# Putting w2 and the later loads behind the DMA transposes of block 1, and letting the scans read their start in place

## The chip, the core and the metric

The kernel runs on one core of a Trainium2 chip. The metric is the device time of one execution in microseconds (us); lower is better. "Span" below is the part of it from the first to the last instruction in the profile; the time is 1.8 to 2.7 us longer than the span in every run listed here. PE is the matmul engine, ACT the scalar engine, DVE the vector engine, POOL is GpSimd, and SP is SyncE, which here only issues DMAs. "Slow" means over 1.5% above the fastest run of the same kernel; every other run is "fast". "Clock" is the share of its full clock that PE was granted, 1.0 being all of it.

## The reference, cut to what matters

```python
xn = layernorm(x)                          # x: [1, 2048, 512] bf16
# A: state-space model. Bu = xn @ B_bar^T (complex), then a scan over 2048 steps
h = Lam_bar * h + Bu[:, t]                 # for each t
ya = 2 * Re(hseq @ C^T) + xn * Dskip
# B: SwiGLU, F = 1792
yb = (silu(xn @ w1) * (xn @ w3)) @ w2
out = x + ya + yb
```

## The kernel before

The 2048 rows are cut into four blocks of 512. For each block the kernel needs xnT, the normalised rows transposed. For blocks 1 to 3 the transposes are DMAs, four of 128 rows each. PE multiplies xnT with w1 and w3 ("gate/up", `glu`), and with B (`bu`). DVE runs the scans. The order of the queue on SP is the order of these calls:

```python
def bulk_loads():                       # called while block 0 starts
    ...
    load_w(4 * P, MID * P)              # slices of w1 and w3
    load_x(1)
    nc.sync.dma_start_transpose(out=bt[:, 0], in_=A_B_re)
    nc.sync.dma_start_transpose(out=bt[:, 1], in_=A_B_im)
    load_w(MID * P, F)
    nc.sync.dma_start_transpose(out=ct_in[:, :, 0, :], in_=A_C_re)
    nc.sync.dma_start_transpose(out=ct_in[:, :, 1, :], in_=A_C_im)
    nc.sync.dma_start(out=w2_sb, in_=...)          # 1792 KB
    nc.sync.dma_start(out=dskip_row, in_=...)

def late_loads():
    load_x(2)
    load_x(3)

def ln_transpose(b, cl):                # blocks 1 to 3
    nc.sync.dma_start_transpose(out=xnT_blk[b][:, :, cl*P:(cl+1)*P], in_=xn_blk[b][:, cl, :])
...
for t in ln1b:                          # normalise block 1 and issue its transposes
    bg.add(*t, ("ln", 1))
bg.add(0.2, params_w)
gate = glu(0)
bg.flush(("ln", 1))
gate()
late_loads()
...
gate = glu(1)                           # first reader of block 1's xnT
```

`bg` is a list of small tasks for the other engines, handed out between PE's groups of matmuls; `flush(key)` empties it up to the last task with that key. The scans of a block start from the last state of the block before. For two of the three hand-overs that state was first copied:

```python
if b == 0: init = 0.0
elif b - 1 in FAST: init = ends[b - 1, hf][:, 2*j + ri : 2*j + ri + 1]
else: init = act_blk[b - 1][:, k_state(pt, ri), TBLK - 1:TBLK]
...
gp.tensor_copy(out=ends[b, hf], in_=act(b)[:, k:k + 4, TBLK - 1])   # after block b's states are done
```

## Time and profile before

| | before |
|---|---|
| time, median of 3 runs | 210.19 us (210.09 to 210.56) |
| the profiled run | 212.91 us, span 210.9 us, state slow |
| PE, DVE, ACT busy | 96%, 86%, 61% of the span |

From the timeline of PE, kernel before (start, length, engine, line, operation, output<-inputs, shapes, count; in brackets the idle time before it and what ended it):

```profile
33.73 5.13 PE L506 MATMUL gu_ps<-xnT,w_sb 128*128 128x512 bf16 x23
41.29 4.02 PE L506 MATMUL gu_ps<-xnT,w_sb 128*128 128x512 bf16 x11 [2.43 <-DMA xnT<-xn]
```

PE ends block 0's gate/up matmuls at 38.86 us (33.73 + 5.13) and stands 2.43 us, until block 1's transposes have landed. The windows of one microsecond show the clock in the third column from the right (PEclk), then DMA share and GB/s:

```profile
39.00:40.00 1.00, 0.00 (x0) 0.00 (x0) 0.96 (x3) 0.50 (x1) 0.00 (x0) 1.00 1.32 259
40.00:41.00 1.00, 0.00 (x0) 0.00 (x0) 1.00 (x2) 0.00 (x0) 0.00 (x0) 0.96 0.80 135
41.00:42.00 1.00, 0.71 (x2) 0.28 (x3) 1.00 (x2) 0.00 (x0) 0.00 (x0) 0.50 0.85 267
42.00:43.00 1.00, 1.00 (x4) 0.34 (x3) 1.00 (x2) 0.00 (x0) 0.00 (x0) 0.50 1.04 310
43.00:44.00 1.00, 1.00 (x4) 0.40 (x3) 1.00 (x2) 0.60 (x1) 0.00 (x0) 0.50 1.04 356
44.00:45.00 1.00, 1.00 (x6) 0.41 (x4) 0.97 (x2) 0.24 (x1) 0.00 (x0) 0.84 0.27 95
```

From shortly before 41 us PE was granted half its clock for 3.4 us (0.08 + 3 + 0.32), a loss of at most 1.7 us: for the first 0.38 us of it PE was still waiting. The queue explains the wait. From the timeline of SP (the length is how long SP was held by issuing, not how long the transfer took: w2, L175, held SP for 0.58 us and landed 9.8 us after its issue):

```profile
20.92 5.74 SPq L173 DMA_TRANSPOSE ct<-in_A_C_re_dram  x1
26.70 2.24 SPq L174 DMA_TRANSPOSE ct<-in_A_C_im_dram  x1
28.99 0.58 SPq L175 DMA_DIRECT2D w_sb<-in_B_w_dram  x1
29.62 1.45 SPq L176 DMA_DIRECT2D dskip_row<-in_A_Dskip_dram  x1
31.17 8.21 SPq L239 DMA_TRANSPOSE xnT<-xn  x4
39.43 1.12 SPq L154 DMA_DIRECT2D x_blk<-in_A_x_dram  x2
```

The normalised rows of block 1 are ready at 25.8 us, but the last of their four transposes is issued at 38.16 and lands at 41.16. The scans, from the page's groups (busy us, mean ns of one, idle before):

```profile
L462 DVE TENSOR_TENSOR_SCAN u<-rho,ends,u 128x512 bf16<-128x512 f32 x16 | 19.6, 1268 | 0.1
L462 DVE TENSOR_TENSOR_SCAN u<-rho,act,u 128x512 bf16<-128x512 f32 x8 | 9.7, 1263 | 0.0
```

### The profile page before, as it was taken

The numbers are of one execution on the slowest core, as the hardware profiler recorded it, in microseconds if no ns is written. First come the engines' busy times: TensorE is split into PE (matmuls) and PEld (weight loads), VectorE is DVE, ScalarE is ACT, GpSimd is POOL, SyncE is SP. The second block draws the span as 40 slices with busy tenths as digits, with TensorE's granted clock in tenths as the row PEclk, the third lists the DMA queues.
The fourth block names the chain that finished last, engine by engine and source line by source line (L and its number), as shares of the span: only waits on it lengthen the run. The fifth ranks groups of instructions, "written<-read, shape, count | busy, mean of one in ns | idle before, by whom it ended". The sixth has DMA issues, their size and how long they took to land.

```text
span 210.9 us, 3257 instructions
## 1 busy us (share of the span) xinstructions
PE 203.2 (96%) x1251; PEld 116.7 (55%) x1251; DVE 181.8 (86%) x236; ACT 128.8 (61%) x257; POOL 28.8 (14%) x51
## 2 busy tenths in 40 slices
PE   8999999599999999999999799999999999999994
PEld 2964444144444444444444344788644448888893
DVE  4789699999893699999999589897999999996932
ACT  4799787369999995727995987401266673011010
POOL 3340399100000003120106000200000000000000
PEclk9999999879999999999999999999999999999999
DMA  5998999930000000440000220000100000001011
GB/s 168 276 177 174 321 238 319 168 133 0 0 3 0 0 0 0 51 120 31 2 0 0 53 50 0 0 28 25 51 3 0 0 0 0 28 25 52 26 39 40
DMA packets 26103, 13.71 MB, mean 65 GB/s; under 512 B 15720, under 2 KB 26088, under 8 KB 26088
## 3 DMA queue, kind: packets, MB, share of 16 engines
q1 hardware_dynamic: 25512, 13.21, 27.5%
q10 hardware_dynamic: 576, 0.30, 0.5%
q8 instruction: 10, 0.16, 0.3%
q14 instruction: 5, 0.04, 0.1%
HBM read 7.74 MB, written 2.10 MB: 47 GB/s over the span
## 4 chain that ended last, share of the span: by engine, by line
PE 74%; DVE 11%; ACT 7%; DMA 3%; POOL 2%; issue 1%; DVEq 0%
PE gu_ps L506 30%; PE gu_ps L697 11%; PE bu_ps L423 8%; PE y_ps L697 7%; PE gu_ps L763 6%; PE bu_ps L697 5%; DMA xnT<-xn 3%; PE bu_ps L190 2%; PE gu_ps L769 2%; DVE u L462 2%; ACT u L516 2%; ACT g L515 1%; DVE act L523 1%; ACT xn L274 1%; DVE stats L211 1%
## 5 line engine op out<-in xcount | busy, mean ns | idle before, releaser
L506 PE MATMUL gu_ps<-xnT,w_sb 128*128 128x512 bf16 x424 | 94.0, 383 | 3.5 <-DMA xnT<-xn 2.4
L506 PEld LDWEIGHTS <-w_sb 128*128 128x128 bf16 x424 | 41.7, 99 | 54.7 <-issue 6.2
L515 ACT ACTIVATE g<-gu_ps 128x512 bf16<-128x512 f32 x55 | 33.1, 602 | 14.2 <-PE gu_ps L506 14.1
L516 ACT ACTIVATE u<-gu_ps 128x512 bf16<-128x512 f32 x55 | 33.3, 605 | 7.5 <-PE gu_ps L506 6.6
L697 PEld LDWEIGHTS <-act 128*128 128x128 f16 x341 | 32.4, 98 | 4.3 <-DVE act L729 0.2
L423 PE MATMUL bu_ps<-xnT,bt 128*128 128x512 bf16 x128 | 28.8, 379 | 0.4 <-DMA xnT<-xn 0.3
L523 DVE TENSOR_TENSOR act<-g,u 128x1024 f16<-128x1024 bf16 x28 | 19.1, 680 | 7.8 <-ACT u L516 7.8
L425 ACT ACTIVATE u<-bu_ps 128x512 bf16<-128x512 f32 x32 | 19.1, 596 | 5.9 <-PE bu_ps L423 5.8
L423 PEld LDWEIGHTS <-bt 128*128 128x128 bf16 x128 | 12.4, 98 | 16.3 <-issue 1.0
L462 DVE TENSOR_TENSOR_SCAN u<-rho,ends,u 128x512 bf16<-128x512 f32 x16 | 19.6, 1268 | 0.1
L763 PE MATMUL gu_ps<-w_sb,act 128*128 128x512 bf16 x56 | 12.4, 379 | 0.0
L447 DVE TENSOR_TENSOR u<-u,tabe 128x2048 bf16<-128x2048 bf16 x8 | 9.8, 1221 | 0.1
L444 DVE TENSOR_TENSOR p<-u,tabe 128x2048 bf16<-128x2048 bf16 x8 | 9.8, 1220 | 0.1
L467 DVE TENSOR_TENSOR p<-u,tabe 128x2048 bf16<-128x2048 bf16 x8 | 9.8, 1220 | 0.1
L474 DVE TENSOR_TENSOR act<-act,p 128x2048 f16<-128x2048 f16 x8 | 9.7, 1216 | 0.1
L451 DVE TENSOR_TENSOR u<-u,p 128x2048 bf16<-128x2048 bf16 x8 | 9.8, 1219 | 0.0
L470 DVE TENSOR_TENSOR act<-u,tabe 128x2048 f16<-128x2048 bf16 x8 | 9.7, 1216 | 0.0
L462 DVE TENSOR_TENSOR_SCAN u<-rho,act,u 128x512 bf16<-128x512 f32 x8 | 9.7, 1263 | 0.0
L282 ACT ACTIVATE xn<-x_blk,acc,rstd_all 128x512 bf16<-128x512 bf16 x8 | 6.2, 811 | 5.3 <-POOL acc L279 5.3
L462 DVE TENSOR_TENSOR_SCAN u<-rho,u 128x512 bf16<-128x512 f32 x8 | 9.2, 1208 | 0.1
L763 PEld LDWEIGHTS <-act 128*128 128x128 f16 x56 | 5.5, 98 | 6.6
L710 ACT ACTIVATE bu_ps<-y_ps 128x256 f32<-128x256 f32 x3 | 1.1, 368 | 11.9 <-PE y_ps L697 11.9
(138 smaller groups left out, 264.0 us busy)
## 6 DMA issues: line engine op xcount, KB each, us to landing
out_dram<-xn SPq DMA_DIRECT2D x15, 128.0 KB, 1.7
w_sb<-in_B_w_dram SPq DMA_DIRECT2D x1, 1792.0 KB, 9.8
x_blk<-in_A_x_dram SPq DMA_DIRECT2D x3, 512.0 KB, 5.5
w_sb<-in_B_w_dram SPq DMA_DIRECT2D x2, 768.0 KB, 6.7
w_sb<-in_B_w_dram SPq DMA_DIRECT2D x4, 256.0 KB, 3.7
w_sb<-in_B_w_dram SPq DMA_DIRECT2D x2, 512.0 KB, 7.6
xnT<-xn SPq DMA_TRANSPOSE x12, 3.0
x_blk<-in_A_x_dram ACTq DMA_DIRECT2D x2, 64.0 KB
```

Of the source, the lines that this page charges most:

```text
L423: nc.tensor.matmul(out=ps, lhsT=bt[:, ri, dt, pt * P:(pt + 1) * P], rhs=xnT_blk[b][:, dt, :], start=(dt == 0), stop=(dt == NDT - 1))
L425: nc.scalar.activation(out=u[:, j, ri, :], in_=ps, func=ACT.Copy)
L444: nc.vector.tensor_tensor(out=st["p"], in0=st["g"], in1=tabe[:, psl, 1:3, :], op=ALU.mult)
L447: nc.vector.tensor_tensor(out=st["g"], in0=st["g"], in1=tabe[:, psl, 0:1, :].to_broadcast(FULL), op=ALU.mult)
L451: nc.vector.tensor_tensor(out=st["g"], in0=st["g"], in1=st["p"][:, :, ::-1, :], op=ALU.subtract)
L462: nc.vector.tensor_tensor_scan(out=v, data0=rho[:, pt:pt + 1].to_broadcast([P, TBLK]), data1=v, initial=init, op0=ALU.mult, op1=ALU.add)
L506: nc.tensor.matmul(out=ps[:, tsl], lhsT=w[:, dt, f * P:(f + 1) * P], rhs=xnT[:, dt, tsl], start=(dt == 0), stop=(dt == NDT - 1))
L515: nc.scalar.activation(out=g16[:, f % 2, :], in_=g_ps, func=ACT.Silu)
L516: nc.scalar.activation(out=u16[:, f % 2, :], in_=u_ps, func=ACT.Copy)
L523: nc.vector.tensor_tensor(out=act(b)[:, k0:k1 + 1:k1 - k0, :], in0=g16, in1=u16, op=ALU.mult)
L697: nc.tensor.matmul(out=out, lhsT=left[:, k, :], rhs=right[k][:, cols], start=(start and k == 0), stop=(k == NK - 1), skip_group_check=True)
L763: nc.tensor.matmul(out=tiles[cl], lhsT=act_blk[b][:, k_gate(f), cl * P:(cl + 1) * P], rhs=w2_sb[:, f, :], start=False, stop=False, skip_gr ...
```

## The change

The intent: in the trace of before the first reader of dskip starts at 54.6 us and the first of w2 at 58.0 us, so let the four transposes of block 1 go ahead of it; and drop the GpSimd copies of the last states. The core of the diff:

```diff
@@ bulk_loads / late_loads
         nc.sync.dma_start_transpose(out=ct_in[:, :, 1, :], in_=A_C_im)
+
+    def late_loads():
         nc.sync.dma_start(out=w2_sb, in_=B_w2.rearrange("(t p) d -> p t d", p=P))
         nc.sync.dma_start(out=dskip_row, in_=A_Dskip.partition_broadcast(P))
-
-    def late_loads():
         load_x(2)
         load_x(3)
@@ scan
-                if b == 0:
-                    init = 0.0
-                elif b - 1 in FAST:
-                    init = ends[b - 1, hf][:, 2 * j + ri:2 * j + ri + 1]
-                else:
-                    init = act_blk[b - 1][:, k_state(pt, ri), TBLK - 1:TBLK]
+                init = 0.0 if b == 0 else act_blk[b - 1][:, k_state(pt, ri), TBLK - 1:TBLK]
@@ post_c
-                if b in FAST and b + 1 < NBLK:
-                    ends[b, hf] = lnp.tile([P, 4], FP16, name="ends", bufs=4)
-                    k = k_state(2 * hf)
-                    gp.tensor_copy(out=ends[b, hf], in_=act(b)[:, k:k + 4, TBLK - 1])
@@ (cut: scans get their own task key, and y_fast flushes it before act is overwritten)
+        if p == 0:
+            bg.flush(("scan", b + 1))
@@ main
     for t in ln1b:
         bg.add(*t, ("ln", 1))
+    bg.add(0.0, late_loads, ("ln", 1))
     bg.add(0.2, params_w)
     gate = glu(0)
     bg.flush(("ln", 1))
     gate()
-    late_loads()
```

Apart from GpSimd's four copies, and the place from which sixteen scans read their start, the programs differ in the order of SP's queue alone. PE, DVE and ACT keep their order.

## The prediction

> **What bounds the kernel now.** The page gives PE 96% busy, DVE 86%, ACT 61%; the chain that ended last is 74% PE. So the time is PE's work plus the places where PE waits or runs slowly. The largest lies between block 0's and block 1's gate/up matmuls. The timeline shows PE idle 2.43 us there (38.86 to 41.29), released by the DMA transposes of block 1 (xnT<-xn). One-microsecond windows then show the granted clock at 0.96, 0.50, 0.50, 0.50, 0.84 from 40 to 45 us: 3.4 us at half speed, which costs half of that, 1.7 us. The chain agrees: the 112 matmuls of block 1 take 25.83 us, those of block 3 24.17 us. The stall costs 2.43 + 1.7 = 4.1 us. [...]
>
> **Why PE waits there.** The normalised x is ready at 25.8 us (timeline of DVE). On SyncE's queue the transposes come after w2 (1792 KB, issued 28.99, 9.8 us to land) and dskip. The first transpose's issue starts at 31.17 and takes 3.85 us; the others take 1.29, 1.57 and 1.22. The last lands at 41.16. Elsewhere too a transpose behind plain copies is slow to issue (9.40, 5.74 us), one behind a transpose is not (2.34, 2.24 us for the big ones).
>
> **What the change does.** The instruction order differs on SyncE only: the four transposes go before w2, dskip and the x loads. GpSimd loses four 128x4 copies; the scans read their start in place.
>
> - Transposes: behind the C transposes, first issue at about 29.0; at 1.2 to 1.6 us each the last is issued at 33 to 34 and lands, at 3.0 us, at 36 to 37. PE wants it at 38.86. The stall goes, with about 2 us to spare, and the half clock with it.
> - Delayed loads: w2, dskip, x2, x3 should land by about 47 us; the first reader (dskip, DVE, now 54.6 us) would come at about 53.
> - Scans: idle before them is 0.1 us; a scan takes 1268 ns from the copy, 1263 ns in place. Worth 0.
>
> **How much stays.** All 4.1 us lie on the chain. DVE is full from 41 to 54 us and uses PE's stall to catch up; its idle time from 53 to 68 us is 0.16 + 0.37 + 0.76 + 2.76 = 4.05 us, just what it must absorb; another 1.78 us follows at 72. The three gate buffers leave over 1 us before ACT would wait. ACT has almost no slack in block 1 (0.6 + 0.6 + 0.7 us busy each 1.73 us). I take off 0.1.
>
> **Prediction.** 210.2 - 4.0 = 206.2 us, 8 in 10 between 205.4 and 207.2. Two per cent is 206.0, so nearly a toss: faster 0.40, same 0.59, slower 0.01.
>
> **What would show it.** The last transpose of block 1 landing before 38.5 us; no PE wait over 0.3 us near 38.9; clock 1.0 from 38 to 46 us; block 1's 112 matmuls in about 24.2 us; DVE idle near zero from 41 to 63 us; block 1 ending near 63 us; later pieces of the chain 4 us earlier, unchanged in length; scans still about 1265 ns.
>
> **What would make it wrong.** The first transpose still issuing slowly (a stall of 0.5 to 1.5 us remains, perhaps without the half clock); DVE's lag filling the gate buffers and holding ACT and PE in block 1; a second clock drop at a later wait, such as the 1.1 us one near 116 us.

## The result, and the profile after

| | before | after |
|---|---|---|
| time, median of 4 runs | 210.14 us (209.93 to 210.56) | 209.06 us (208.91 to 209.37) |
| ratio of fast runs | | 0.9948, 95% interval 0.9928 to 0.9968 |
| the profiled run | 212.91 us, span 210.9, slow | 209.37 us, span 207.5, fast |

A ratio here is the mean time of one kernel's fast runs over the mean of the other's fast runs of the same rounds, so it isn't quite the ratio of the medians. The change is a gain of 0.5%, where 2% had been expected, and 209.06 lies outside the predicted 205.4 to 207.2.

Yet the profile after shows almost everything that was predicted. Timelines of SP and PE, changed kernel:

```profile
24.63 2.41 SPq L174 DMA_TRANSPOSE ct<-in_A_C_im_dram  x1
27.15 6.56 SPq L239 DMA_TRANSPOSE xnT<-xn  x4
33.76 0.57 SPq L177 DMA_DIRECT2D w_sb<-in_B_w_dram  x1
34.39 0.92 SPq L178 DMA_DIRECT2D dskip_row<-in_A_Dskip_dram  x1
35.35 2.20 SPq L154 DMA_DIRECT2D x_blk<-in_A_x_dram  x2
```

```profile
33.66 8.58 PE L497 MATMUL gu_ps<-xnT,w_sb 128*128 128x512 bf16 x38
```

The transposes go first; the trace's landing records have the last of them at 34.94 us, 4.7 us before PE wants it at 39.66. PE runs through without a gap. Two of the windows, and the stretch that was DVE's worry:

```profile
40.00:41.00 1.00, 1.00 (x6) 0.41 (x5) 0.97 (x3) 0.73 (x2) 0.00 (x0) 1.00 1.09 325
42.00:43.00 1.00, 1.00 (x7) 0.45 (x5) 1.00 (x2) 1.00 (x3) 0.00 (x0) 1.00 1.04 365
41.00:63.00 22.00, 21.89 (x101) 9.96 (x102) 21.83 (x23) 21.27 (x39) 0.00 (x0) 1.00 0.17 51
```

The clock is 1.00, PE is busy 21.89 of 22 us, DVE 21.83 of 22: it has used up its idle time, as predicted, and holds nobody. The scans:

```profile
L456 DVE TENSOR_TENSOR_SCAN u<-rho,act,u 128x512 bf16<-128x512 f32 x24 | 29.3, 1268 | 0.0
```

One thing is different from before: early, at 9.8 us, PE waits for a slice of the weights, which the profiled run of before did not.

```profile
9.79 0.40 PE L528 MATMUL bu_ps<-xnT,w_sb 128*128 128x128 bf16 x4 [0.78 <-DMA w_sb<-in_B_w_dram]
```

So the two profiles differ by 3.3 us of span and the median times by 1.1 us. The profile of before is of a slow run, that of after is not, and the two must not be compared. That is the first thing to look into.

### The profile page after: what moved, and what is told of

The parts are those of the page before. It is cut to its first block, busy times and chain, and to the rows that moved or that the text cites. A ratio compares the mean times of both kernels' runs of the same rounds, so it can differ in the third digit from the quotient of the medians.

```text
span 207.5 us, 3235 instructions
## 1 busy us (share of the span) xinstructions
PE 200.8 (97%) x1237; PEld 116.0 (56%) x1251; DVE 181.6 (87%) x236; ACT 128.8 (62%) x257; POOL 25.5 (12%) x47
## 4 chain that ended last, share of the span: by engine, by line
PE 84%; ACT 6%; DMA 5%; POOL 1%; issue 1%; DVE 1%; ACTq 0%; POOLq 0%
PE gu_ps L497 39%; PE gu_ps L690 11%; PE bu_ps L422 11%; PE y_ps L690 7%; PE gu_ps L756 6%; PE bu_ps L690 6%; DMA w_sb<-in_B_w_dram 2%; PE gu_ps L762 2%; DMA x_blk<-in_A_x_dram 2%; ACT xn L274 1%; ACT u L424 1%; DMA xnT<-xn 1%; ACT u L507 1%; ACT g L506 1%; POOL rstd_all L278 1%
## 5 line engine op out<-in xcount | busy, mean ns | idle before, releaser
L497 PE MATMUL gu_ps<-xnT,w_sb 128*128 128x512 bf16 x415 | 91.7, 379 | 1.6 <-ACT g L506 1.1
L456 DVE TENSOR_TENSOR_SCAN u<-rho,act,u 128x512 bf16<-128x512 f32 x24 | 29.3, 1268 | 0.0
L703 ACT ACTIVATE gu_ps<-gu_ps 128x256 f32<-128x256 f32 x3 | 1.1, 368 | 11.7 <-PE gu_ps L690 11.7
```

The lines of the kernel that those rows point to most:

```text
L456: nc.vector.tensor_tensor_scan(out=v, data0=rho[:, pt:pt + 1].to_broadcast([P, TBLK]), data1=v, initial=init, op0=ALU.mult, op1=ALU.add)
L497: nc.tensor.matmul(out=ps[:, tsl], lhsT=w[:, dt, f * P:(f + 1) * P], rhs=xnT[:, dt, tsl], start=(dt == 0), stop=(dt == NDT - 1))
```

## The experiments

Theory A: the profile of before was no typical run. Its DMAs ran late, so the wait was long and the half clock followed; a typical run of before loses only about 1 us. Rival B: the wait is 2.4 us in every run, only the half clock is missing in fast ones, and the changed kernel gives 1.3 us back elsewhere. Rival C: part of the gain comes from the scans.

### e1: the kernel before, unchanged, in a fast run

No edit.

> The kernel before, unchanged, for profiles and clocks of fast runs (the profile that the prediction was read from was a run of 212.9 us, the median is 210.1). Theory A (the profile before was not a typical run: there the stream of DMAs ran about 2.3 us late before the changed part began, so the wait at 38.9 us was long and the half clock followed): a fast run has clock near 1.0, no half-clock stretch of 3.4 us, PE's wait for the transposes of block 1 is 0.3 to 1.5 us, time 210.1. Rival B (the wait is about 2.4 us in fast runs too, only the half clock is missing, and the changed kernel gives 1.3 us back elsewhere): PE's wait there is 2.1 to 2.7 us at clock 1.0.

Measured: 209.72 us (209.03 to 211.38, 6 runs), all fast, clocks 0.998 to 1.0. The profiled run took 209.96 us, with a span of 207.9 us at clock 1.0. Timelines of PE and SP:

```profile
29.79 9.44 PE L506 MATMUL gu_ps<-xnT,w_sb 128*128 128x512 bf16 x43
39.86 5.34 PE L506 MATMUL gu_ps<-xnT,w_sb 128*128 128x512 bf16 x24 [0.62 <-ACT u L516]
```

```profile
25.46 2.22 SPq L174 DMA_TRANSPOSE ct<-in_A_C_im_dram  x1
27.73 0.58 SPq L175 DMA_DIRECT2D w_sb<-in_B_w_dram  x1
28.35 1.31 SPq L176 DMA_DIRECT2D dskip_row<-in_A_Dskip_dram  x1
29.77 8.18 SPq L239 DMA_TRANSPOSE xnT<-xn  x4
```

PE's gap is 0.62 us and the clock stays up. The profile puts the gap down to ACT's u, which ran from 39.27 to 39.88 us; but in the changed kernel the same u ran from 39.69 to 40.29 us while PE went on without a gap. The last transpose, issued at 36.72, landed after 3.0 us at 39.72, and PE went on at 39.86, 0.14 us later (0.13 us in the slow run, 41.16 to 41.29). Here w2 was issued at 27.73, in the slow run at 28.99, and PE arrived 0.4 us later. Theory A holds on this run, and B's 2.1 to 2.7 us is not there. The windows at the wait, with the clock third from the right:

```profile
39.00:40.00 1.00, 0.38 (x3) 0.13 (x2) 0.98 (x2) 0.60 (x2) 0.00 (x0) 1.00 0.51 116
40.00:41.00 1.00, 1.00 (x6) 0.45 (x5) 0.99 (x1) 0.08 (x1) 0.00 (x0) 1.00 1.07 379
```

The same program's ratio to itself in these rounds was 0.9987 (0.9938 to 1.0035), which shows how far noise alone can move a ratio.

The traces allow a stricter test. PE loads its weights 1251 times in the same order in both kernels, so the same load can be found in each trace. Work it out for three landmarks (times from the trace's weight-load records, us):

| trace | first 512-column load | block 0 after `bu` + all gate/up of block 1 | from `bu` of block 1 to the end of the span | span |
|---|---|---|---|---|
| before (slow) | 12.53 | 38.61 | 144.12 | 210.85 |
| e1, before (fast) | 12.90 | 35.32 | 144.10 | 207.91 |
| after | 13.32 | 34.53 | 144.08 | 207.53 |

Between the first two columns lie 15.59 us in all three. So all differences sit in two places: how early the first weights let PE start, and the stretch with the wait. 34.53 us is that stretch without a wait: the slow run of before loses 4.08 us in it, as the prediction had it, and the fast run loses 0.79. The changed kernel gives nothing back later: B's second half falls as well. (The last stretch is not always that constant. In the traces of e5, e8 and e10 it takes 143.73 to 143.75 us, 0.35 us less. In e8, which is the changed kernel once more, the difference begins where `bu` of block 2 waits for block 2's transposes.)

### e2 and e3: the two halves of the change, one at a time

e2 is the kernel before with only the load order changed (the first and the last part of the diff above). e3 has only the scans and the copies changed.

> Only the loads moved behind the transposes; the GpSimd copies of the last states stay. Theory A: the whole gain, 209.0 to 209.2 us (ratio 0.9945 to 0.996), PE's wait at 39 us gone. Rival C (part of the gain is from the scans): 209.5 us or more.

> Only the scans read the last states in place, loads as before. Theory A: as before, 210.0 to 210.3 us (ratio 0.999 to 1.001), scan mean 1260 to 1270 ns. Rival C: 209.7 us or less.

Measured: e2 took 209.12 us (208.68 to 209.52), ratio 0.9948 (0.9903 to 0.9993), the whole of the gain; its stretch is 34.53 us, as in the changed kernel. e3 took 210.28 us (208.29 to 213.58, two of six runs slow), ratio of the fast runs 0.9957 (0.9893 to 1.0022). That interval is too wide to tell anything, and its point misses the expected 0.999 to 1.001; leaving out the two slow runs also flatters it. The trace decides in its place: from `bu` of block 1 on, where the scans in question run, e3 takes 144.10 us, like e1. The in-place read is worth nothing on PE's path, and C falls. e3 has the old load order, so its trace is a second fast one of that order: PE waits 1.01 us there, and the stretch with the wait takes 35.70 us, 1.17 more than without a wait.

```profile
40.75 9.44 PE L497 MATMUL gu_ps<-xnT,w_sb 128*128 128x512 bf16 x43 [1.01 <-DMA xnT<-xn]
```

e3's own spread shows what the old load order does: spans of 206.5, 206.5, 207.1, 208.8, 209.6 and 211.2 us, the last at clock 0.992. So the half clock does come in the old order, now and then: in this run and in the profiled run of before, and in none of the 39 runs that are counted below.

### e4 and e9: a larger dose of the old order

```diff
         nc.sync.dma_start(out=dskip_row, in_=A_Dskip.partition_broadcast(P))
-
-    def late_loads():
         load_x(2)
         load_x(3)
...
     gate()
-    late_loads()
```

Against the kernel before, the loads of x blocks 2 and 3 (1 MB) also go ahead of the transposes.

> The reverse of the change, as a dose: the loads of x blocks 2 and 3 (1 MB, about 3.2 us at the 320 GB/s seen in this stretch) also go before the transposes. Theory A: the wait at 39 us grows to 3.5 to 5 us, and now the half clock of 3.4 us follows in most runs (1.7 us): 214 to 216 us. If a long wait by itself does not bring the half clock: 212.8 to 213.8 us at clock 1.0. Rival B: the wait is about 5.6 us.

> e4 again, for a count: there the half clock followed the 3.8 us wait in two of four runs. [...] again some runs at clock 0.992 and span 211 to 212, the others at 1.0 and 209.5 to 210.2; both kinds seen.

Measured: e4 213.02 us (212.28 to 214.21, 4 runs), e9 215.43 us (212.00 to 216.51, 6 runs, three of them slow). PE's wait in e4's profiled run, and two windows of it:

```profile
42.42 3.91 PE L504 MATMUL gu_ps<-xnT,w_sb 128*128 128x512 bf16 x11 [3.78 <-DMA xnT<-xn]
```

```profile
41.00:42.00 1.00, 0.00 (x0) 0.00 (x0) 1.00 (x2) 0.00 (x0) 0.00 (x0) 0.91 0.82 149
43.00:44.00 1.00, 1.00 (x4) 0.29 (x2) 1.00 (x1) 0.00 (x0) 0.00 (x0) 0.50 0.00 0
```

The wait grows with what is put ahead. The ten runs fall into three kinds: clock 1.0 with spans of 209.8, 209.9 and 210.0 us; clock 0.992 with 211.1, 211.8, 212.3 and 212.8; clock 0.984 with 213.5, 214.3 and 214.5. The steps fit one and two half-clock stretches of 1.7 us, though only the 0.992 kind has a trace. e4's median came out below the expected 214 to 216 us, as half of its runs had no half clock; five of e9's six spans (212.3 to 214.5 us) are above the expected 211 to 212, three of them with what looks like two stretches. And the half clock is not fixed by the length of the wait: e9's profiled run waited 3.17 us and kept its clock, the slow run of before waited 2.43 us and lost it.

```profile
41.91 4.26 PE L504 MATMUL gu_ps<-xnT,w_sb 128*128 128x512 bf16 x19 [3.17 <-DMA xnT<-xn]
```

The clock records of the traces say more about when. All changes of clock lie a whole number of steps of 3.413 us after the first rise to the full clock in the same trace: 34.134 us (10 steps) in the slow run of before, 37.547 us (11) in e4, 204.800 us (60) in e9, where PE's work was over. The half clock in the slow run of before lasted 3.413 us, one step. Cut each trace into windows at these steps. The clock fell at the end of a window in which PE had stood for 2.05 us (slow run of before, window ending at 40.91) or 3.19 us (e4, ending at 41.83). e9's wait of 3.17 us fell across the boundary at 40.59, 1.84 us in one window and 1.32 in the next, and the clock stayed. In the ten traces with clock records (all but e1 and e3, where no change was recorded) the clock fell after every window with 2.05 us idle or more and after none with 1.84 us or less. So in these traces it is the idle time within one window that counts, and where a wait falls decides. (The ends of matmuls in the profile are modelled. All these idle times may be about 0.2 us too short, an estimate from e1's gap of 0.62 us, which cost 0.79 us.)

### e5 and e10: keep PE busy in the wait

```diff
     gate()
+    spin = ps_bu.tile([P, TBLK], FP32, name="bu_ps")
+    for _ in range(14):
+        nc.tensor.matmul(out=spin, lhsT=ones[:, 0:P], rhs=ones, start=True, stop=True)
```

This goes on top of e4; the dummy results are read by nobody.

> The dose kernel e4 (x blocks 2 and 3 also ahead of the transposes) with 14 dummy matmuls (3.0 us) on PE in the wait. In e4 two of four runs had the half clock (spans 211.8 and 211.1 us), two had not (209.8, 209.9). If the half clock comes from PE standing idle: no run at 0.992, all spans 209.3 to 210.4 us, time 211.6 to 212.8. If it comes from something else (the DMAs, the phase of the run alone): spans near 211.5 us again in about half the runs.

> e5 again, for a count: with the dummy matmuls in the wait none of four runs had the half clock. If idleness of PE is what brings it, none of these six has it either (all spans 209.3 to 210.6 us); if the four were luck, about three of six at 0.992.

Measured: 212.62 us (212.28 to 212.88, 4 runs) and 212.75 us (211.70 to 213.75, 6 runs). In e5's trace the transposes come as late as in e4 (PE goes on at 42.51 us, there at 42.42), but PE's gap is 0.74 us:

```profile
38.55 3.22 PE L805 MATMUL bu_ps<-const-bfloat16-1.0 128*128 128x512 bf16 x14
42.51 7.71 PE L504 MATMUL gu_ps<-xnT,w_sb 128*128 128x512 bf16 x34 [0.74 <-DMA xnT<-xn]
```

Not one of the ten runs has a clock below 1.0, against seven of ten without the dummies. (Some of e10's spans, up to 211.2 us, are above the expected 210.6: the wait itself varies.) The last comparison is within the same rounds for e9 and e10: five of six runs against none of six. The DMAs issued were the same; so in these runs it is PE standing idle that brings the half clock. It also says what the dummies are worth: they keep the clock, not the time of the wait, and removing the wait is better.

### e6: is it the place in the queue, or the bytes?

```diff
+    def load_w2():
+        nc.scalar.dma_start(out=w2_sb, in_=B_w2.rearrange("(t p) d -> p t d", p=P))
     def late_loads():
-        nc.sync.dma_start(out=w2_sb, in_=B_w2.rearrange("(t p) d -> p t d", p=P))
         nc.sync.dma_start(out=dskip_row, in_=A_Dskip.partition_broadcast(P))
...
+    bg.add(0.0, load_w2)
     for t in ln1b:
         bg.add(*t, ("ln", 1))
```

This is the changed kernel with w2 in ACT's DMA queue, issued at 20.53 us. In SP's queue nothing but transposes stands ahead of block 1's from 19.8 us on.

> The changed kernel, but w2 alone is issued on ACT's DMA queue, at about 20 us, so it is in flight together with the C transposes and ahead of the block-1 transposes in time, but not ahead of them in SyncE's queue. If only the place in the queue counts: the last block-1 transpose is done by 36 us, no PE wait, spans as e8. [...] the transposes of C and of block 1 finish 3 to 6 us later than in the changed kernel (33 to 34.4 us by packets), 37 to 40 us, and PE waits 0 to 1.5 us.

(The second case is that w2's bytes delay the transposes although they are in another queue.)

Measured: 211.71 us (211.25 to 212.99, 4 runs, the longest at clock 0.992), ratio to before 1.0089. PE's wait of 1.77 us, and the last packet at 40.64 us, are a little over what was expected. Timelines of SP and PE:

```profile
19.81 5.81 SPq L173 DMA_TRANSPOSE ct<-in_A_C_re_dram  x1
25.66 8.35 SPq L174 DMA_TRANSPOSE ct<-in_A_C_im_dram  x1
34.11 5.77 SPq L241 DMA_TRANSPOSE xnT<-xn  x4
```

```profile
41.35 1.89 PE L499 MATMUL gu_ps<-xnT,w_sb 128*128 128x512 bf16 x8 [1.77 <-DMA xnT<-xn]
```

The second C transpose held SP for 8.35 us, where it took 2.24, 2.22 and 2.41 us in the other traces shown. It stood behind a transpose in its own queue each time; only here was w2 moving in the other queue. The packets of block 1's last transpose end at 40.64 us against 34.48 in the changed kernel. From 25 to 31 us the packet records show 1579 packets of the C transposes beside 1435 of w2. In the slow run of before, with both in SP's queue, block 1's transposes have no packet from 30.74 to 36.09 us, while w2's and dskip's pass. So another queue was no way out for a w2 issued at 20.53 us: it moved beside the transposes, and they ended 6.16 us later than in the changed kernel (40.64 against 34.48 us). In the changed kernel w2 is issued at 33.76 us, behind the transposes, and PE does not wait. How w2 in the other queue held the transposes back was not shown.

### e8 and e7: the changed kernel again, and one more wait removed

e8 is the changed kernel without edit. e7 adds an empty slot to the list of block 3's normalisation on ACT, so that ACT goes on emptying PSUM for PE while GpSimd computes the scale:

```diff
         for fn in (total, squares, norm):
+            if fn is norm and spread is not None:
+                spread.append((None, lambda: None))
             for cl in range(CPB):
```

> The changed kernel, unchanged, on the same chip as the kernels below. From the three landmarks of the traces so far, span = 194.2 + (time at which the third weight slice lets PE go on, 12.3 to 13.4 us) + (PE's wait for the transposes of block 1) + 1.7 if the half clock follows. Theory A: here the wait is 0 in every run, so spans 206.5 to 207.6 us and a narrow spread (highest minus lowest time under 1.2 us), where the kernel before spreads over 2 to 3 us; ratio 0.990 to 0.998.

> The changed kernel with one empty slot between the squares and the normalisation of block 3, so that ACT evacuates block 2's matmuls while GpSimd works out the scale (there ACT stood 2.6 us and PE 1.1 us, in every trace of either kernel, block 2 taking 25.43 us against 24.07 us of block 3). Expected: block 2 in 24.1 to 24.5 us, perhaps up to 0.5 us back as a wait for block 3's transposes; 0.8 to 1.3 us faster than the changed kernel, near 208.0 us, ratio to the kernel before 0.985 to 0.991. Rival: the wait only moves to the transposes of block 3 and the time stays at 209.1.

Measured: e8 208.99 us (208.59 to 209.98), ratio to before 0.9954 (0.9918 to 0.999), spans 206.6 to 207.6; its highest minus lowest time, 1.39 us, is a little over the expected 1.2. The kernel before, in the same rounds, ran from 209.06 to 211.52 us. e7 took 207.84 us (207.22 to 210.31), ratio to before 0.991 (0.9862 to 0.9959). ACT's wait for GpSimd, changed kernel first, then e7:

```profile
112.77 0.81 ACT L282 ACTIVATE xn<-x_blk,acc,rstd_all 128x512 bf16<-128x512 bf16 x1 [2.57 <-POOL acc L279]
```

```profile
112.06 0.81 ACT L282 ACTIVATE xn<-x_blk,acc,rstd_all 128x512 bf16<-128x512 bf16 x1 [0.84 <-POOL acc L279]
```

By the weight-load records, block 2's gate/up matmuls take 24.17 us in e7 instead of 25.43, and no wait for block 3's transposes appears. The mean of e7's six times is 208.17 us, that of e8's 209.09. e7 is faster than the kernel before; that it is faster than the changed kernel rests on the traces (142.85 us from `bu` of block 1 to the end, against 144.09 and, in e8, 143.73), as six times that spread over 3.1 us can't tell 0.9 us for sure. One of e7's runs, of 210.31 us, has no trace and stays unexplained.

## Why the prediction was wrong

- **"The stall costs 2.43 + 1.7 = 4.1 us"** is the step that failed. As a reading of that one trace it was right: 4.08 us by landmarks. (In part by luck. The wait cost some 2.6 us, as a gap in this place costs 0.17 us more than it shows: 0.62 and 0.79 in e1. The half clock cost some 1.5, half of the 3.04 us from 41.29 to 44.33 us, as it began 0.38 us before PE went on. The two errors cancel.) As the cost in the runs that were timed it was wrong. The trace was of a run of 212.91 us; the median was 210.19. I took the loss from the slow run and subtracted it from the fast ones. From its own run it gives 212.9 - 4.1 = 208.8 us, close to the 209.06 measured.
- **What stood in its place:** the 39 runs of the unedited kernel before in the rounds of e1, e8 and e9 (e1's own six among them), all fast, have a mean span of 207.72 us, and the ten of the changed kernel 206.93. The stall is worth about 0.8 us there; the two fast traces of the old order show 0.79 (e1) and 1.17 (e3). None of the 39 has a clock below 0.998, so the half clock, some 1.5 of the 4.1 us, is not in them; and PE's wait is 0.62 us in the one fast trace and 1.01 in the other, in place of 2.43. (The clocks of the four runs of before in the result's own rounds are not on record; the 39 stand for them.)
- **"All 4.1 us lie on the chain" and nothing is given back:** right in kind. The rest of the kernel is the same to 0.04 us (144.08 to 144.12) in the three traces of the table, and 0.35 us shorter in e8, so each microsecond of wait removed there is a microsecond of span.
- **Transposes landing at 36 to 37, with 2 us to spare:** better than predicted, 34.94 us and 4.7 us to spare. PE wait gone, clock 1.0, as predicted.
- **Block 1's matmuls in about 24.2 us, DVE idle near zero, the gate buffers not in the way:** right (34.53 us for the whole stretch in after, e2, e7 and e8; DVE 21.83 of 22 us).
- **Block 1 ending near 63 us:** 63.8 us, because this run started 0.8 us later, at the wait for the weights at 9.8 us. In the old order a late start should be partly hidden, as PE then comes later to the same wait for the transposes, while in the new order it shows in full; no run tested this alone.
- **Scans worth 0:** right by the traces; the timing of e3 alone could not have told.
- **A transpose is slow to issue behind plain copies, fast behind a transpose:** it fitted the trace of before (9.40, 5.74 and 3.85 us behind plain copies, 2.34 and 2.24 us behind a transpose), but the neighbour in the queue is not reason enough. e6 has a transpose behind a transpose that took 8.35 us.
- **Delayed loads landing by about 47 us, dskip's first reader at about 53:** the loads were done at 45.0 us by packets; the reader came at 55.1 us in a run that started 0.8 us later, so DVE, full here, gained some 0.2 us and not 1.6.

What stays open is why the DMAs' progress differs by a microsecond or two between runs of the same program: it is seen in the traces (the last of block 1's transposes ends at 39.06 us by packets in e1, 39.84 in e3, 40.53 in the slow run), and no run tested a cause. The spans of the old order ran from 206.5 to 209.3 us in the 39 fast runs, those of the new order from 206.5 to 207.6 in ten.

## What to carry to other kernels

Before you price a stall from a profile, compare the profiled run's own time with the median you will subtract from. If it is slower, the stall you see may be the reason for just that, and the typical run has less of it. Load in the order of need, and don't count on another queue: here w2 (1792 KB, wanted at 58 us), started early, went with a wait of PE for block 1's transposes from their own queue (0.62, 1.01 and 2.43 us in e1, e3 and the slow run of before) and from ACT's (1.77 us, e6). And a wait for DMAs cost more than its length where PE's clock fell after it (2.43 us of wait, 4.08 us lost, in the slow run of before), but only in some runs (seven of the ten of e4 and e9): count the runs.
